# Decode attention on one core: last K block in partition quarters, last turns moved, more of wo before the last V half

## Chip, cores, metric

The kernel runs on 1 core of one Trainium2 chip. The metric is the device time of one execution in microseconds (us), lower is better; quoted times are medians.

## The reference

One decode step: a single query against a long K and V cache, beside a small gated feed-forward part. Cut to what matters here:

```python
# H = 16 heads, Sk = 65536 keys, Dh = 256, D = 448, all bf16
q = (xn @ wq).reshape(B, Sq, H, Dh).transpose(0, 2, 1, 3)
scores = einsum("bhqd,bhkd->bhqk", q, k_cache) * (Dh ** -0.5)
p = softmax(scores, axis=-1)
o = einsum("bhqk,bhkd->bhqd", p, v_cache)
s = o.transpose(0, 2, 1, 3).reshape(B, Sq, H * Dh) @ wo
out = x + s * silu(ffn(xn))          # [1, 1, 448]
```

K and V are 537 MB each. Nearly all the work is to read them once.

## The kernel before

The cache is cut into 64 blocks (16 heads, 4 blocks each) of 128 partitions x 128 keys, 8.4 MB of K and as much of V. Three buffers R0, R1, R2 take the K and V blocks in turn. VectorE and ScalarE form the scores of a block, TensorE multiplies the softmax weights with V, and SyncE issues all large loads into one queue (q1 in the page: 1084.30 of 1084.52 MB). Blocks run in loops; the last ones are written out after them. The parts that the change touches:

```python
def load_keys(T, src, k0, k1, s):
    w = slice(k0 * Dh, k1 * Dh)
    sp.dma_start(out=T[:, w], in_=src[:, w]).then_inc(s, 16)

# after SyncE's loop: K63, V62, V63 and wo, all in one queue
take(sp, vf[0])                                # TensorE has finished with V60 in R0
load_keys(R[0], Kl, 0, HK, kl[0])              # K63, keys 0-63, all 128 partitions
load_keys(R[0], Kl, HK, KB, kh[0])             # K63, keys 64-127
take(sp, kf[2])
for (k0, k1), w in zip(vn, nl):                # V62 in 4 parts
    load_keys(R[2], Vn, k0, k1, w)
take(sp, vf[1])
for (k0, k1), w in zip(vz[:2], zl[:2]):        # V63, first half
    load_keys(R[1], Vl, k0, k1, w)
take(sp, kf[0])                                # VectorE is done with K63's first half
load_wo(0); load_wo(1)                         # wo goes where that half was
for (k0, k1), w in zip(vz[2:], zl[2:]):        # V63, second half
    load_keys(R[1], Vl, k0, k1, w)
load_wo(2); load_wo(3)
# ... (cut)
# TensorE and ScalarE at the end (cut to the order)
keys(psO2, 0, 1, vz, zl, 0, 2, True, od)       # V63 first half
pe_turn()                                      # turns V62's output
project(*pieces[0]); pe_rows(); project(h0, h0 + 3); pe_bcast(); project(h0 + 3, h1)
# ... softmax of the second half, sums, weights
keys(psO, 0, 1, vz, zl, 2, 3, True)
pe_turn()                                      # turns the output of V63's first half
keys(psO, 0, 1, vz, zl, 3, len(vz), False, od)
project(*pieces[2]); pe_turn(tok=True); project(pieces[3][0], H1); project(H1, H)
```

A "turn" is 8 small matmuls that transpose a finished output row; `project` multiplies finished heads with their part of wo.

Of the kernel before, what the change touches and what calls it, by code (L numbers as in the profile page):

```python
# [14 lines left out]
KB = 128  # L15
# [6 lines left out]
def kernel(  # L22
# [25 lines left out]
    LAST = NBLK - 1  # L48
# [19 lines left out]
    pe, dve, act, gp, sp = nc.tensor, nc.vector, nc.scalar, nc.gpsimd, nc.sync  # L68


    KW, HK = KB * Dh, KB // 2

    R = [pool.tile([P, KW], bf16, name=f"R{t}") for t in range(NR)]
# [32 lines left out]
    def rest(n0, n):  # L106
        return R[2][:, n0 : n0 + n], n0 + n

    wq_t, n = rest(0, DF * HD + HD // 2)
    Z, n = rest(n, DX * H * H)  # L110
    w1_t, n = rest(n, DF * F + F // 2)
    w2_t, n = rest(n, FC * D)
    xn, n = rest(n, D)
    xz, n = rest(n, 2 * P)
# [11 lines left out]
    psO, ps_m, ps_nb, ps_t = bank[0][0:2, :], bank[1][:, 0:P], bank[2][:, 0:1], bank[3][:, 0:2]  # L126
    ps_q, ps_y, ps_ao, ps_tot = bank[4][:, 0:Dh], bank[5][0:1, 0:D], bank[6][0:1, 0:D], bank[7]
    psO2, ps_qh = bank[4][0:2, :], bank[3][0:H, 0:Dh]
# [10 lines left out]
    def mark(e, ins):  # L139
        count[e] += 1  # L140
        ins.then_inc(line[e], 1)
        return (e, count[e])

    def need(e, *toks):
        for p, c in toks:
            if seen.get((e, p), 0) < c:
                eng[e].wait_ge(line[p], c)
                seen[(e, p)] = c

    def sem(name):  # L150
        return tc.alloc_semaphore(name)

    def take(e, s, k=1):
        e.wait_ge(s, k).then_inc(s, -k)  # L154

    kl = [sem(f"kl{t}") for t in range(NR)]
    kh = [sem(f"kh{t}") for t in range(NR)]
# [7 lines left out]
    od, oc, ho = sem("od"), sem("oc"), sem("ho")  # L165
# [3 lines left out]
    def cuts(*c):  # L169
        return tuple(zip(c[:-1], c[1:]))  # L170

    vn = cuts(0, 32, 64, 96, 128)
    vz = cuts(0, 32, 64, 96, 112, 120, 128)
    nl = [sem(f"nl{t}") for t in range(len(vn))]
    zl = [sem(f"zl{t}") for t in range(len(vz))]
    pieces = cuts(0, 5, 10, 14, 16)
    wl = [sem(f"wl{t}") for t in range(len(pieces))]

    Kd = A_k_cache[0].rearrange("h (b p c) d -> (h b) p (c d)", p=P, c=KB)
# [3 lines left out]
    def at(n):  # L183
        return slice(n, n + 1) if isinstance(n, int) else bass.ds(n, 1)

    def block(T, i):
        return T[at(i)].rearrange("o p f -> (o p) f")
# [11 lines left out]
# [3 lines that stand above are left out]
# [10 lines left out]
    def dve_gmax():  # L212
        take(dve, tm)
        dve.reduce_max(out=gmax[0:1, :], in_=ps_m[0:1, :], axis=AX.X).then_inc(gm, 1)  # L214


    def dve_block(s, between=None):
        Kv = R[s][:, :].rearrange("p (c d) -> p c d", d=Dh)


        def end(c0, c1, own):
            take(dve, pf, (c1 - c0) // SUB)
            take(dve, sd, own)
            dve.tensor_copy(out=S2[:, c0:c1], in_=S[:, c0:c1]).then_inc(kf[s], 1)  # L224
            dve.reduce_max(out=rmax[:, :], in_=S[:, c0:c1], axis=AX.X).then_inc(rm, 1)  # L225
            if c0 == 0 and between:
                between()
            dve_gmax()

        take(dve, qr)  # L230
        dve.tensor_copy(out=qcur[:, :], in_=ps_q).then_inc(sd, 1)  # L231
        halves = between is not None
        take(dve, kl[s], 16)
        for k in range(NSTEP):
            if k == NSTEP // 2:
                take(dve, kh[s], 16)
            pair = Kv[:, k * SUB + ND : (k + 1) * SUB, :]
            m = dve.tensor_tensor(  # L238
                out=pair,
                in0=pair,  # L240
                in1=qcur[:, None, :].to_broadcast([P, NA, Dh]),
                op=ALU.mult,
            )
            if k == 0:
                m.wait_op(sd, 1, "sem-ge")
            m.then_inc(mr, 1)
            for j in range(ND):
                c = k * SUB + j
                ins = dve.tensor_tensor_reduce(  # L249
                    out=Kv[:, c, :],  # L250
                    in0=Kv[:, c, :],
                    in1=qcur[:, :],
                    scale=1.0,
                    scalar=0.0,
                    op0=ALU.mult,
                    op1=ALU.add,
                    accum_out=S[:, c : c + 1],
                )
            if k == NSTEP - 1:
                ins.then_inc(sd, 1)  # L260
                end(KB // 2 if halves else 0, KB, 1 if halves else 2)
            elif halves and k == NSTEP // 2 - 1:
                ins.then_inc(sd, 1)
                end(0, KB // 2, 2)

    def act_sums(s, k):
        take(act, mr)
        for j in range(NA):
            c = k * SUB + ND + j
            prod = R[s][:, c * Dh : (c + 1) * Dh]  # L270
            ins = act.activation(  # L271
                out=prod,
                in_=prod,
                func=ACT.Identity,
                accum_out=S[:, c : c + 1],
            )
        ins.then_inc(pf, 1)

    def act_softmax(e, s, c0=0, c1=KB):
        def col(a, b):  # L280
            return hist[:, at(e + 2), a:b].rearrange("p o s -> p (o s)")

        take(act, bm)
        act.mul(out=col(0, 1), in_=ps_nb, mul=-scale).then_inc(sa, 1)  # L284
        take(act, sa)
        act.activation(  # L286
            out=PV[s][:, c0:c1],
            in_=S2[:, c0:c1],
            func=ACT.Exp,
            bias=col(0, 1),  # L290
            scale=scale,
            accum_out=col(1, 2),
        ).then_inc(pv, 1)

    def act_out(po=psO):
        take(act, od)
        act.copy(out=O[:, :], in_=po).then_inc(oc, 1)  # L297
# [5 lines left out]
    def act_row(e):  # L303
        take(act, ho)
        return act.copy(out=hist[:, at(e + 2), 2:4].rearrange("p o s -> p (o s)"), in_=ps_t)  # L305
# [35 lines left out]
    def pe_turn(tok=False):  # L341
        take(pe, oc)
        Ov = O[:, :].rearrange("r (j p a) -> r j a p", j=2, a=2)
        for a in range(2):
            for j in range(2):
                ins = pe.matmul(  # L346
                    ps_t[:, a : a + 1],
                    lhsT=Ov[:, j, a, :],
                    rhs=eye2[:, j : j + 1],
                    start=(j == 0),  # L350
                    stop=(j == 1),
                )
        return mark("pe", ins) if tok else ins.then_inc(ho, 1)
# [36 lines left out]
    with tc.tile_critical():  # L390
# [18 lines left out]
        Kl, Vn, Vl = block(Kd, LAST), block(Vd, LAST - 1), block(Vd, LAST)  # L409
# [3 lines left out]
            sp.dma_start(out=wo_t[:, h0:h1, :], in_=wo_d[:, h0:h1, :]).then_inc(w, 16)  # L413

        take(sp, vf[0])
        load_keys(R[0], Kl, 0, HK, kl[0])
        load_keys(R[0], Kl, HK, KB, kh[0])
        take(sp, kf[2])
        for (k0, k1), w in zip(vn, nl):
            load_keys(R[2], Vn, k0, k1, w)  # L420
# [18 lines left out]
        for T, w in ((ident, P), (eye2, 2)):  # L439
# [19 lines left out]
        t = mark("dve", dve.tensor_scalar(  # L459
            out=xn,  # L460
            in0=x_f[0:1, :],
            scalar1=mv[0:1, 0:1],
            scalar2=rstd,
            op0=ALU.subtract,
            op1=ALU.mult,
        ))
# [50 lines left out]
        t = mark("pe", ins)  # L517
# [165 lines left out]
        def keys(po, t, s, cut, sems, a, b, start, done=None):  # L683
            for n in range(a, b):
                (k0, k1), last = cut[n], n == b - 1
                pe.wait_ge(sems[n], 16)
                pe_keys(po, t, s, k0, k1, start and n == a, last and done is not None,
                        done if last else None)
# [3 lines left out]
        keys(psO, 2, 2, vn, nl, 3, 4, False, od)  # L692
        pe_bcast()
        act_softmax(LAST, 0, 0, HK)
        act_sums(0, 2)
        act_out()
        act_sums(0, 3)
        act_row(LAST - 1)


        take(pe, pv)
        keys(psO2, 0, 1, vz, zl, 0, 2, True, od)
        pe_turn()
        need("pe", t_o)
        pe.wait_ge(wl[0], 16)
        project(*pieces[0])
# [3 lines left out]
        project(h0, h0 + 3)  # L710
        pe_bcast()
        project(h0 + 3, h1)
        act_softmax(LAST + 1, 0, HK, KB)

        take(pe, pv)
        t15 = pe_sums(ps_m[:, 0:NL], N1, NENT)
        weights(N1, NENT, H1, H, (ps_m[:, 0:NL], t15))
        act_out(psO2)
        keys(psO, 0, 1, vz, zl, 2, 3, True)
        pe_turn()  # L720
        t_g = silu(g_t, ps_y, g_e, t_y)
        t = mark("act", act_row(LAST))
        need("dve", t)
        outputs(N1, NENT - 1, H1, H, NL - 1)
        keys(psO, 0, 1, vz, zl, 3, len(vz), False, od)
        act_out()
        pe.wait_ge(wl[2], 16)
        project(*pieces[2])
        t = pe_turn(tok=True)
# [12 lines left out]
        t = mark("pe", project(H1, H))  # L742
        need("dve", t, t_g)
        t = mark("dve", dve.tensor_tensor(out=g_t, in0=ps_ao, in1=g_t, op=ALU.mult))  # L744
        need("dve", t)
        t = mark("dve", dve.tensor_tensor(  # L746
            out=x_f[0:1, :], in0=g_t, in1=x_f[0:1, :], op=ALU.add
        ))
# [32 lines left out]
```

## Time and profile before

| | before |
|---|---|
| time, median of the first 3 runs | 2525.48 us |
| span of the profiled run | 2523.2 us |
| read from HBM | 1084.29 MB, 430 GB/s over the span |
| K63: from first issue to last landing | 23.2 us |
| last K63 landing to the end of TensorE's last matmul | 53.3 us |
| VectorE's pause before block 63 | 6.8 us |

K63 was issued at 2442.65 and had landed at 2465.85; TensorE's last matmul ended at 2519.14. The prediction below shows the DMA row of the page, the chain of waits and the ends of the timelines. The table by stretches of time, here while K63 loads (stretch, length, busy time of each engine, granted TensorE clock, busy share of the DMA engines, GB/s):

```profile
2447.00:2460.00 13.00, 12.17 (x59) 4.88 (x57) 10.75 (x52) 8.76 (x44) 0.00 (x0) 1.00 0.95 410
```

TensorE's timeline at the first matmuls on V62 (start, length, engine, line, what, count, and in brackets the idle time before and what ended it):

```profile
2460.84 1.07 PE L346 MATMUL bank<-eye,O 2*128 2x1 f32 x8 [1.30 <-PEq L154]
2470.98 9.37 PE L318 MATMUL bank<-R,PV 128*2 128x512 bf16 x32 [9.08 <-DMA R<-in_A_v_cache_dram]
```

K63 passes at 410 GB/s, and TensorE waits 9.08 us for V62, which is queued behind it.

### The profile page before, as it was taken

Reading aid. Unit: us, or ns where it says so; the run is one execution under the profiler, and the core shown is the slowest. Engines: PE = TensorE matmul, PEld = TensorE weight load, DVE = VectorE, ACT = ScalarE, POOL = GpSimd, SP = SyncE. Lnnn points to the kernel's source line nnn. Section 1 sums busy time; section 2 is a strip of 40 time slices with the busy share of each in tenths; the row PEclk is TensorE's granted clock in tenths of the full one; section 3 lists DMA queues with packets and bytes.
Section 4 is the critical chain, followed back from the end, with each engine's and each line's share of the span. In section 5 each row is a group of like instructions: output and inputs, shape, how many; then the busy total and the mean of one; then the engine's idle time right before and its main releaser. Section 6 shows DMA issues by size and latency. Waiting matters only on the chain. (4 is left out here: it accounts for less than half of the span.)

```text
span 2523.2 us, 29918 instructions
## 1 busy us (share of the span) xinstructions
PE 1198.1 (47%) x5125; PEld 500.5 (20%) x5125; DVE 2233.7 (89%) x10281; ACT 1443.9 (57%) x6992; POOL 2.5 (0%) x13
## 2 busy tenths in 40 slices
PE   3353543534535435445354354454553543534556
PEld 2121211212212112112121121221221211212222
DVE  6989889889899898898898988988989889889886
ACT  3656556556555565565565655655656556556554
POOL 0000000000000000000000000000000000000000
PEclk7676767767767767677676676676766767767778
DMA  9999999999999999999999999999999999999998
GB/s 423 417 430 433 434 431 433 433 432 432 432 432 432 433 434 437 434 435 433 433 433 432 432 432 432 432 433 434 439 434 433 433 433 433 432 432 432 432 412 346
DMA packets 22728, 1084.52 MB, mean 430 GB/s; under 512 B 2354, under 2 KB 4532, under 8 KB 4916
## 3 DMA queue, kind: packets, MB, share of 16 engines
q1 hardware_dynamic: 22706, 1084.30, 99.5%
q8 instruction: 6, 0.10, 0.0%
q14 instruction: 14, 0.11, 0.0%
q10 hardware_dynamic: 2, 0.00, 0.0%
HBM read 1084.29 MB, written 0.00 MB: 430 GB/s over the span
## 5 line engine op out<-in xcount | busy, mean ns | idle before, releaser
L271 ACT ACTIVATE R<-R 128x256 bf16<-128x256 bf16 x3328 | 1330.7, 401 | 697.1 <-ACTq L154 697.1
L249 DVE CUSTOM_DVE_ANT_0 R<-R,qcur 128x256 bf16<-128x256 bf16 x4864 | 1700.2, 417 | 0.0
L318 PE MATMUL bank<-R,PV 128*2 128x512 bf16 x4096 | 1023.7, 416 | 32.4 <-DMA R<-in_A_v_cache_dram 15.3
L238 DVE TENSOR_TENSOR R<-R,qcur 128x3328 bf16<-128x3328 bf16 x256 | 482.6, 1885 | 198.7 <-DVEq L154 198.6
L271 ACT ACTIVATION_READ_ACCUMULATOR R<-R 128x1 f32 x3328 | 620.2, 186 | 2.6 <-issue 2.6
L330 PE MATMUL bank<-ident,rmax 128*1 128x128 bf16 x65 | 17.1, 263 | 1021.6 <-PEq L154 1021.6
L318 PEld LDWEIGHTS bank<-R,PV 128*2 128x2 bf16 x4096 | 365.0, 90 | 663.1 <-issue 208.0
L249 DVE DVE_READ_ACCUMULATOR2_ANT S<- 128x1 f32 x4864 | 383.5, 79 | 0.0
L346 PE MATMUL bank<-eye,O 2*128 2x1 f32 x536 | 98.0, 300 | 236.8 <-PEq L154 236.8
L330 PEld LDWEIGHTS bank<-ident,rmax 128*1 128x1 bf16 x65 | 5.2, 79 | 1026.1 <-issue 1025.9
L346 PEld LDWEIGHTS bank<-eye,O 2*128 2x128 f32 x536 | 94.2, 257 | 254.8 <-issue 254.8
L284 ACT ACTIVATE hist<-bank 128x1 f32 (+1 forms) x65 | 11.1, 171 | 203.4 <-ACTq L154 203.4
L305 ACT COPY hist<-bank 128x2 f32 (+1 forms) x66 | 10.5, 160 | 120.0 <-ACTq L154 120.0
L214 DVE TENSOR_REDUCE gmax<-bank 1x1 bf16<-1x128 f32 x65 | 18.2, 281 | 36.2 <-DVEq L154 36.2
L231 DVE CAST qcur<-bank 128x256 bf16<-128x256 f32 x64 | 27.2, 425 | 20.2 <-DVEq L154 18.3
L297 ACT COPY O<-bank 2x512 f32<-2x512 f32 x67 | 37.5, 559 | 9.1 <-ACTq L154 9.1
L286 ACT ACTIVATE PV<-S,hist 128x128 bf16<-128x128 f32 (+1 forms) x65 | 26.0, 400 | 13.4 <-ACTq L154 13.1
L358 PE MATMUL bank<-q,ident 16*128 16x256 bf16 x63 | 24.4, 387 | 0.0
L224 DVE COPY S<-S 128x128 f32<-128x128 f32 (+1 forms) x65 | 14.7, 226 | 9.5
L225 DVE TENSOR_REDUCE rmax<-S 128x1 bf16<-128x128 f32 (+1 forms) x65 | 18.2, 279 | 0.0
L336 PE MATMUL bank<-gmax,ones_row 1*128 1x1 bf16 x65 | 10.3, 158 | 15.9 <-PEq L154 15.9
L336 PEld LDWEIGHTS bank<-gmax,ones_row 1*128 1x128 bf16 x65 | 6.5, 99 | 33.3 <-issue 33.3
(65 smaller groups left out, 101.7 us busy)
## 6 DMA issues: line engine op xcount, KB each, us to landing
R<-in_A_k_cache_dram SPq DMA_DIRECT2D x4, 4096.0 KB, 23.4
R<-in_A_v_cache_dram SPq DMA_DIRECT2D x7, 2048.0 KB, 23.1
R<-in_A_wq_dram SPq DMA_DIRECT2D x1, 3072.0 KB, 12.7
R<-in_A_wo_dram SPq DMA_DIRECT2D x2, 1120.0 KB, 17.5
R<-in_B_w_dram SPq DMA_DIRECT2D x1, 1568.0 KB, 27.2
R<-in_B_w_dram SPq DMA_DIRECT2D x1, 1344.0 KB, 5.8
R<-in_A_v_cache_dram SPq DMA_DIRECT2D x1, 1024.0 KB, 15.8
R<-in_A_v_cache_dram SPq DMA_DIRECT2D x2, 512.0 KB, 17.0
```

The lines of the kernel that those rows point to most:

```text
L214: dve.reduce_max(out=gmax[0:1, :], in_=ps_m[0:1, :], axis=AX.X).then_inc(gm, 1)
L225: dve.reduce_max(out=rmax[:, :], in_=S[:, c0:c1], axis=AX.X).then_inc(rm, 1)
L231: dve.tensor_copy(out=qcur[:, :], in_=ps_q).then_inc(sd, 1)
L238: m = dve.tensor_tensor(out=pair, in0=pair, in1=qcur[:, None, :].to_broadcast([P, NA, Dh]), op=ALU.mult,)
L249: ins = dve.tensor_tensor_reduce(out=Kv[:, c, :], in0=Kv[:, c, :], in1=qcur[:, :], scale=1.0, scalar=0.0, op0=ALU.mult, op1=ALU.add, accum ...
L271: ins = act.activation(out=prod, in_=prod, func=ACT.Identity, accum_out=S[:, c : c + 1],)
L286: act.activation(out=PV[s][:, c0:c1], in_=S2[:, c0:c1], func=ACT.Exp, bias=col(0, 1), scale=scale, accum_out=col(1, 2),).then_inc(pv, 1)
L297: act.copy(out=O[:, :], in_=po).then_inc(oc, 1)
L318: ins = pe.matmul(po, lhsT=PV[t][:, c : c + 2], rhs=R[s][:, c * Dh : (c + 2) * Dh], start=(start and c == k0), stop=(stop and c == k1 - 2),)
L330: pe.matmul(ps_m[0:1, :], lhsT=rmax[:, 0:1], rhs=ident[:, :], start=True, stop=True).then_inc(tm, 1)
L346: ins = pe.matmul(ps_t[:, a : a + 1], lhsT=Ov[:, j, a, :], rhs=eye2[:, j : j + 1], start=(j == 0), stop=(j == 1),)
L358: pe.matmul(ps_q, lhsT=ident[0:H, at(h)].to_broadcast([H, P]), rhs=q16[:, :], start=True, stop=True,).then_inc(qr, 1)
```

## The change

The intent, as I read it: shorter transfers of K63, so that other traffic gets between them; and less work for TensorE after the last V part lands, by doing turns and projections in its earlier pauses. Loops and arithmetic are unchanged.

```diff
--- before.py
+++ after.py
@@ -170,10 +170,12 @@
         return tuple(zip(c[:-1], c[1:]))
 
     vn = cuts(0, 32, 64, 96, 128)
-    vz = cuts(0, 32, 64, 96, 112, 120, 128)
+    vz = cuts(0, 32, 64, 80, 96, 112, 120, 128)
     nl = [sem(f"nl{t}") for t in range(len(vn))]
     zl = [sem(f"zl{t}") for t in range(len(vz))]
-    pieces = cuts(0, 5, 10, 14, 16)
+    pieces = cuts(0, 5, 12, 14, 16)
+
+    kr = cuts(0, 32, 64, 96, 128)
     wl = [sem(f"wl{t}") for t in range(len(pieces))]
 
     Kd = A_k_cache[0].rearrange("h (b p c) d -> (h b) p (c d)", p=P, c=KB)
@@ -230,10 +232,11 @@
         take(dve, qr)
         dve.tensor_copy(out=qcur[:, :], in_=ps_q).then_inc(sd, 1)
         halves = between is not None
-        take(dve, kl[s], 16)
+        n = 16 * len(kr) if halves else 16
+        take(dve, kl[s], n)
         for k in range(NSTEP):
             if k == NSTEP // 2:
-                take(dve, kh[s], 16)
+                take(dve, kh[s], n)
             pair = Kv[:, k * SUB + ND : (k + 1) * SUB, :]
             m = dve.tensor_tensor(
                 out=pair,
@@ -413,8 +416,9 @@
             sp.dma_start(out=wo_t[:, h0:h1, :], in_=wo_d[:, h0:h1, :]).then_inc(w, 16)
 
         take(sp, vf[0])
-        load_keys(R[0], Kl, 0, HK, kl[0])
-        load_keys(R[0], Kl, HK, KB, kh[0])
+        for (c0, c1), sm in zip(cuts(0, HK, KB), (kl[0], kh[0])):
+            for p0, p1 in kr:
+                load_keys(R[0][p0:p1, :], Kl[p0:p1, :], c0, c1, sm)
         take(sp, kf[2])
         for (k0, k1), w in zip(vn, nl):
             load_keys(R[2], Vn, k0, k1, w)
@@ -692,15 +696,18 @@
         keys(psO, 2, 2, vn, nl, 3, 4, False, od)
         pe_bcast()
         act_softmax(LAST, 0, 0, HK)
+        act_out()
         act_sums(0, 2)
-        act_out()
+        act_row(LAST - 1)
         act_sums(0, 3)
-        act_row(LAST - 1)
 
 
         take(pe, pv)
-        keys(psO2, 0, 1, vz, zl, 0, 2, True, od)
+        keys(psO2, 0, 1, vz, zl, 0, 1, True)
         pe_turn()
+        keys(psO2, 0, 1, vz, zl, 1, 2, False, od)
+        act_out(psO2)
+        act_softmax(LAST + 1, 0, HK, KB)
         need("pe", t_o)
         pe.wait_ge(wl[0], 16)
         project(*pieces[0])
@@ -710,19 +717,16 @@
         project(h0, h0 + 3)
         pe_bcast()
         project(h0 + 3, h1)
-        act_softmax(LAST + 1, 0, HK, KB)
+        pe_turn()
 
         take(pe, pv)
         t15 = pe_sums(ps_m[:, 0:NL], N1, NENT)
         weights(N1, NENT, H1, H, (ps_m[:, 0:NL], t15))
-        act_out(psO2)
-        keys(psO, 0, 1, vz, zl, 2, 3, True)
-        pe_turn()
+        t_r = mark("act", act_row(LAST))
         t_g = silu(g_t, ps_y, g_e, t_y)
-        t = mark("act", act_row(LAST))
-        need("dve", t)
+        need("dve", t_r)
         outputs(N1, NENT - 1, H1, H, NL - 1)
-        keys(psO, 0, 1, vz, zl, 3, len(vz), False, od)
+        keys(psO, 0, 1, vz, zl, 2, len(vz), True, od)
         act_out()
         pe.wait_ge(wl[2], 16)
         project(*pieces[2])
```

## The prediction

> **What bounds the kernel now.** I read four views of the kernel before, widest first. The page shows what fills the span:
>
> ```profile
> DMA  9999999999999999999999999999999999999998
> HBM read 1084.29 MB, written 0.00 MB: 430 GB/s over the span
> L249 DVE CUSTOM_DVE_ANT_0 R<-R,qcur 128x256 bf16<-128x256 bf16 x4864 | 1700.2, 417 | 0.0
> ```
>
> All 40 slices of the DMA row are full. VectorE is busy for 89% of the span, but it too waits for transfers. The diff touches nothing in the loops, so only the last 80 us, after K block 63 is issued, can move. The chain of work that ended last, in order of time (start, us, what), says what ends the program:
>
> ```profile
> 2484.34 23.09 DMA R<-in_A_v_cache_dram
> ...
> 2507.47 3.61 PE bank L318 x16
> 2511.08 1.03 PE bank L346 x8
> 2512.11 3.54 PE bank L318 x16
> 2515.66 1.51 PE bank L662 x8
> 2517.17 1.03 PE bank L346 x8
> 2518.20 0.95 PE bank L662 x4
> ...
> 2519.18 0.62 DVE R L744
> 2519.82 0.61 DVE x_f L746
> ```
>
> The last V half lands while wo is still arriving; then TensorE alone needs 11.67 us (3.61+1.03+3.54+1.51+1.03+0.95) to 2519.15, VectorE 1.23, and the output transfer 2.8 to the span's end at 2523.2. Third, the timelines of VectorE and TensorE in that stretch:
>
> ```profile
> 2458.56 0.28 DVE L214 TENSOR_REDUCE gmax<-bank 1x1 bf16<-1x128 f32 x1 [0.94 <-DVEq L154]
> 2465.61 0.42 DVE L231 CAST qcur<-bank 128x256 bf16<-128x256 f32 x1 [6.77 <-DVEq L154]
> ...
> 2503.67 0.22 PE L330 MATMUL bank<-ident,rmax 128*1 128x128 bf16 x1 [0.49 <-PEq L154]
> 2507.47 3.61 PE L318 MATMUL bank<-R,PV 128*2 128x512 bf16 x16 [0.99 <-DMA R<-in_A_v_cache_dram]
> ```
>
> VectorE stands 6.77 us between block 62 and block 63. It does not wait for data: the query matmul (L358) ended at 2458.62, and the two K63 transfers, issued from 2442.65, landed after 12.0 and 22.8 us, so the first half was in SBUF at 2454.65. Fourth, the line view of L201 there, and the DMA queues from 2463.7 to 2465.7:
>
> ```profile
> DMA to landing us min/median/max: 12.0/17.4/22.8
> ...
> q14 instruction: 1, 0.01, 1.0%
> ```
>
> From 2458.7 to 2463.7 that view shows only the data queue. One 8 KB instruction transfer runs at 2463.76, just as an engine ends its rows of the second K63 half, and VectorE resumes 1.5 us after it. I read the stall as an instruction fetch after the loop[...].
>
> [...] a 128-partition K63 half gives each engine 8 rows of 32 KB at 1.213 us (from the transfer records), 9.7 us in a row, and the fetch enters at its end.
>
> [...] The trace before has no transfer of 32 partitions that could test this; it shows only the full rate, 32 KB in 1.213 us on each of 16 engines, 432 GB/s[...].[...]
>
> **The change part by part.**
>
> 1. Quarters of K63: two transfers of 4 MB become eight of 1 MB. At 0.38 us per issue this adds 6 x 0.38 = 2.3 us to SyncE, which next has work at 2457.5: hidden. [...] 8.39 MB take 38.8 us instead of 19.4 (8.39 MB / 432 GB/s). Everything behind is in the same queue: V62 (8.39 MB), V63 (8.39), wo (3.67). It arrives 19 us later.
>
> VectorE barely cares: the first half would land at 2443.6 + 19.4 = 2463, before it now starts (2465.6), and the second at 2482, where it starts the second half at 2486.2. The cost sits purely on the transfers.
>
> 2. More wo early: piece 1 grows from 5 to 7 heads. Two heads are 2 x 229 KB = 0.46 MB, 1.07 us at 430 GB/s. All later V63 parts land 1.07 us later; the last wo byte is unmoved. Four projection matmuls (about 0.85 us) leave the end.
>
> 3. Smaller first parts of the last V half: 32 keys (4.9 us of transfer) become 16+16. The first lands 2.44 us earlier than the 32 would, 1.37 net of part 2. One more issue (about 0.45 us), hidden, SyncE being some 17 us ahead.
>
> 4. Turns: V62's turn moves between the parts of V63's first half, and that half's turn (1.03 us) moves from the final stretch into the wait for the last half. ScalarE's copies move ahead to suit. The number of matmuls does not change.
>
> At full rate the sum is: wo piece 1 lands at 2502.5 + 1.07 = 2503.6; TensorE then runs its 14 projection matmuls (2.9), a turn (1.0), and the sums (0.4), to about 2508.0. The first 16 keys landed at 2506.0, so it runs 32 key matmuls of 0.2255 back to back: 7.2, to 2515.2. Then four projections 0.85, turn 1.03, last projections 0.95: 2518.0, instead of 2519.15. That is 1.1 us. VectorE restarting some 3.7 us sooner (2458.8 + 1.2 mean wait + 0.3 + 1.5 = 2461.9, not 2465.6) gives TensorE at most 0.5 more before landings bind. So parts 2 to 4 with a shorter fetch are worth 1 to 2 us: 2524.
>
> At half rate: the last wo piece, issued at about 2496.8 and landed 19.1 us later at 2515.9, lands at about 2515.9 + 19 = 2534.9. TensorE has caught up with its transfers by then; after the landing there are 0.95 of projections, 1.23 of VectorE and 2.8 of output, so the span ends at 2539.9, 16.7 above 2523.2. About 2.4 us of the old chain thus hides under the delay. Some lag of single engines at the old end (1 to 3 us between the first engine and the last) may go, so I take 15.5: 2541.
>
> **The rivals.**
>
> A, my main case: the eight quarters run at half rate in turn, 2541. [...] Against: [...] whoever split by partition rather than by key must have expected something of it.
>
> B: quarters cost nothing[...]. Then the fetch gets in sooner and the tail shrinks: 2524. For it: the 6.77 us stall is real[...]. Against: VectorE's restart is not on the chain that ended last; the 23.09 us transfer is. So even then little comes of it.
>
> C: partial overlap. The engines start K63 staggered by up to 0.7 us and may drift apart[...]. With 300 GB/s K63 takes 28 us, 8.6 late; TensorE's 3 us of backlog absorbs part, and the time is about 2531.
>
> D: the fetch stays as long[...]. This changes VectorE by 2 to 3 us, but with A's delay nothing at the end.
>
> **Range and chances.** I give A 0.62, B 0.26, C 0.12. A spans 2537 to 2545, B 2522.5 to 2525.5. A range for eight in ten must hold both, 2522.5 to 2544; the centre is weighted to A with a little of C: 2538. Either way it is well under 2% (50 us): faster 0.005, same 0.985, slower 0.01.
>
> **What would show each step.** Right under A: the K63 quarters of the first half land up to some 20 us after issue and the second up to 39; a stretch from 2444 to 2482 shows about 215 to 230 GB/s; TensorE's first V62 matmul moves from 2470.98 to about 2489; the chain ends in a wait for wo or the last V part, followed by only a few matmuls. Right under B: the same stretch shows 430 GB/s, the cast at L231's successor starts at about 2462, TensorE's last matmul ends at about 2518, and the chain keeps about 32 key matmuls after the last wait. A new idle of TensorE before a turn or the projections would show step 4 wrong. The prediction as a whole fails if the quarters cost more than half the rate, or if the time falls below 2522.

Three things stand as assumptions. First, that quarters of 32 partitions run at half rate: 38.8 us is twice the 19.4 that the trace gives for K63. On it the sum of case A came to a span of 2539.9, 16.7 us above 2523.2, and with 15.5 in place of 16.7 to a time of 2541. Second, that a fetch enters once an engine has ended its rows of one transfer, as the one fetch seen did. With quarters the longest wait would then be two rows of 1.213 us, 2.4 us; half of it is the "1.2 mean wait" in the full-rate sum, which came to 2518.0 for TensorE's end and 2524 for the time. Third, in rival D, that the fetch waits as long as before because two rows at half rate take 4.9 us.

## The result

The changed kernel takes 2545.13 us (2543.87 to 2547.67, 6 runs) against 2525.47 (2525.04 to 2528.47, 6 runs). The ratio is 1.0077, 95% interval 1.0064 to 1.009. The change costs some 20 us, clearly, though less than the 2% that counts as slower. The prediction was 2538 with a range up to 2544: the right direction and the right class, 1.1 us outside the range.

The page of the changed kernel. The DMA row and the GB/s row have one figure for each fortieth of the span:

```profile
DMA  9999999999999999999999999999999999999998
GB/s 419 415 428 431 431 435 436 430 433 439 431 429 436 438 429 433 439 431 430 438 435 429 434 439 430 429 442 432 429 436 437 430 431 441 431 429 440 433 284 337
HBM read 1084.29 MB, written 0.00 MB: 426 GB/s over the span
```

The DMA row is the same, digit for digit, as before. The loss shows only in GB/s: slice 39 falls to 284, where the kernel before has 412. The same stretch in the table by stretches:

```profile
2447.00:2460.00 13.00, 13.00 (x62) 5.05 (x61) 11.83 (x59) 10.25 (x52) 0.00 (x0) 1.00 0.97 202
```

The DMA engines are as busy as before (0.97 against 0.95) and move half as much (202 GB/s against 410). In the transfer records a row of 32 KB takes 2.55 us in place of 1.213 (medians of K63's 256 rows). The eight K63 loads, from issue to landing in the line view of L203, where the two of before took 12.0 and 22.8 us:

```profile
DMA to landing us min/median/max: 7.6/24.4/40.4
```

The timeline of VectorE, then that of TensorE (the line numbers are 2 or more higher than before):

```profile
2460.59 0.28 DVE L216 TENSOR_REDUCE gmax<-bank 1x1 bf16<-1x128 f32 x1 [1.62 <-DVEq L154]
2470.54 0.42 DVE L233 CAST qcur<-bank 128x256 bf16<-128x256 f32 x1 [9.66 <-DVEq L154]
...
2506.97 0.28 DVE L216 TENSOR_REDUCE gmax<-bank 1x1 bf16<-1x128 f32 x1 [13.68 <-DVEq L154]
```

```profile
2493.38 13.39 PE L321 MATMUL bank<-R,PV 128*2 128x512 bf16 x48 [29.43 <-DMA R<-in_A_v_cache_dram]
...
2518.72 5.30 PE L321 MATMUL bank<-R,PV 128*2 128x512 bf16 x16 [1.12 <-DMA R<-in_A_v_cache_dram]
2523.86 2.06 PE L666 MATMUL bank<-R,OT 128*1 128x448 bf16 x10
2525.75 0.22 PE L333 MATMUL bank<-ident,rmax 128*1 128x128 bf16 x1
2525.87 1.30 PE L666 MATMUL bank<-R,OT 128*1 128x448 bf16 x6
2527.10 0.17 PE L339 MATMUL bank<-gmax,ones_row 1*128 1x1 bf16 x1
2527.20 1.68 PE L666 MATMUL bank<-R,OT 128*1 128x448 bf16 x8
2528.80 1.10 PE L349 MATMUL bank<-eye,O 2*128 2x1 f32 x8
2529.83 0.39 PE L653 MATMUL bank<-hist,ones_sq 128*128 128x5 f32 x2
2530.15 7.07 PE L321 MATMUL bank<-R,PV 128*2 128x512 bf16 x32
2537.05 0.92 PE L666 MATMUL bank<-R,OT 128*1 128x448 bf16 x4
2538.05 1.07 PE L349 MATMUL bank<-eye,O 2*128 2x1 f32 x8
2539.05 1.01 PE L666 MATMUL bank<-R,OT 128*1 128x448 bf16 x4
```

TensorE now waits 29.43 us for V62 instead of 9.08. VectorE's pause before block 63 grew from 6.77 to 9.66 us, and a new one of 13.68 appeared: its next step needs a small TensorE matmul (L333, at 2506.61) that stands behind the late V62 keys (2493.38 to 2506.77) in TensorE's order. At the end, once the last bytes of V63's first half have come (2518.72), TensorE's matmuls run to 2540.06 without any pause. Their first 16 took 5.30 us instead of 3.61 before, at a granted clock of 0.68 in that stretch against 1.00. Even so TensorE was not late at the end: the weight load (PEld) of the four projections at 2537.05 still had to wait for a part of wo:

```profile
2537.00 0.52 PEld L666 LDWEIGHTS bank<-R,OT 128*1 128x1 bf16 x4 [0.29 <-DMA R<-in_A_wo_dram]
```

The profiled spans differ by 2544.16 - 2523.24 = 20.9 us. I split this at the landings of K63:

| stretch, us | before | after | difference |
|---|---|---|---|
| start of the span to the first K63 issue | 2442.65 | 2444.68 | +2.0 |
| K63 issue to last K63 landing | 23.2 | 43.75 | +20.55 |
| last K63 landing to the end | 57.38 | 55.73 | -1.65 |

The first row lies before anything that the change touches; it is the spread between two executions. The medians, which average over it, differ by 19.7.

### The profile page after: what moved, and what is told of

It reads as the page before. It is cut to its first block, busy times and chain, and to the rows that moved or that the text cites. A ratio compares the mean times of both kernels' runs of the same rounds, so it can differ in the third digit from the quotient of the medians. Undisturbed runs are those within 1.5% of the kernel's fastest.

```text
span 2544.2 us, 29925 instructions
## 1 busy us (share of the span) xinstructions
PE 1204.5 (47%) x5125; PEld 502.8 (20%) x5125; DVE 2233.6 (88%) x10281; ACT 1443.5 (57%) x6992; POOL 2.5 (0%) x13
## 5 line engine op out<-in xcount | busy, mean ns | idle before, releaser
L333 PE MATMUL bank<-ident,rmax 128*1 128x128 bf16 x65 | 17.1, 263 | 1019.2 <-PEq L154 1019.2
L333 PEld LDWEIGHTS bank<-ident,rmax 128*1 128x1 bf16 x65 | 5.2, 79 | 1023.5 <-issue 1023.1
```

Of the source, the lines that this page charges most:

```text
L333: pe.matmul(ps_m[0:1, :], lhsT=rmax[:, 0:1], rhs=ident[:, :], start=True, stop=True).then_inc(tm, 1)
```

## The experiments

**Theory and rivals.** My theory: a transfer over 32 or 64 neighbouring partitions runs at half rate, one over 16 at a quarter, one over partitions spread over the whole range at the full rate, and nothing overlaps a slow one. No trace had shown why that should be so; it is an assumption that the runs test. In the expectations below, the forecast before each rival is the theory's. Rivals: small or numerous transfers are slow; the order of the quarters is at fault; the loss needs the other parts of the change. A second question is what the instruction fetch behind VectorE's pause waits for (that the pause is such a fetch is my reading; in all twelve traces an 8 KB instruction transfer runs in it and VectorE goes on 1.5 to 2.0 us after its end). The fetch theory is the prediction's second assumption: it enters where an engine has ended its rows of one transfer, since the one in the trace before ran at 2463.76, just after the first such ends (2463.62). A third question is what parts 2 to 4 are worth. Ten kernels ran, all correct. The first four shared one chip and 9 runs of the kernel before (2526.32); the second four another and 7 runs (2526.65); the last two one run (2526.26).

### Quarters undone, the rest kept

```diff
-    kr = cuts(0, 32, 64, 96, 128)
+    kr = cuts(0, 128)
```

> The changed kernel with only the quarters undone: each half of K block 63 is again one transfer over all 128 partitions. [...] K63 again takes about 20 us at 430 GB/s and the time is 2524, 1 to 2 us below the kernel before. Rival (the rest of the change costs time, for instance the reordered turns or the larger wo piece): the time stays several us above the kernel before, 2530 or more.

Measured: 2525.03 us, ratio 0.9996 (0.9983 to 1.001), which the interval does not tell from no change. K63 took 23.3 us. The whole loss is in the quarters. In the trace, last K63 landing to TensorE's end is 52.0 us against 53.3 before: the rest of the change does save about 1.3 us there, too little for the runs to show.

### Quarters alone, on the kernel before

```diff
-        load_keys(R[0], Kl, 0, HK, kl[0])
-        load_keys(R[0], Kl, HK, KB, kh[0])
+        for (c0, c1), sm in zip(cuts(0, HK, KB), (kl[0], kh[0])):
+            for p0, p1 in kr:
+                load_keys(R[0][p0:p1, :], Kl[p0:p1, :], c0, c1, sm)
     # and the waits of 16 on kl[0], kh[0] become 16 * len(kr)
```

> The kernel before with only the quarters added. [...] K63 takes some 42 us, as in the changed kernel, and the time is 2545 to 2547, at or 1 to 2 us above the changed kernel because the old end of the program is kept. Rival (quarters are harmless alone, the loss needs the new order): 2525.

Measured: 2545.85 us, ratio 1.0077 (1.0061 to 1.0092), the same as the whole change. From the last K63 landing to TensorE's end it took 51.75 us, as good as the changed kernel's 51.6: in these two executions the old end is in total no worse than the new. In this execution K63 was issued 5 us earlier, behind a V61 that was still loading, so issue to landing (48.6) is not comparable; the last byte landed at 2485.96, 20.1 later than before.

### Same number of transfers, cut by keys instead of partitions

```diff
-            for p0, p1 in kr:
-                load_keys(R[0][p0:p1, :], Kl[p0:p1, :], c0, c1, sm)
+            for t in range(len(kr)):
+                w = (c1 - c0) // len(kr)
+                load_keys(R[0], Kl, c0 + t * w, c0 + (t + 1) * w, sm)
```

> The changed kernel with each K63 half cut into four transfers of 16 keys over all 128 partitions instead of four of 32 partitions: as many transfers, of the same 1 MB each. [...] full rate, 430 GB/s over K63, time 2523 to 2525. Rival (eight small transfers, or two waits for four, cost the time): about 2545 as in the changed kernel. Fetch theory[...]: VectorE's pause before block 63 shrinks from 6.8 us to 5 or less, because an engine has 2.4 us of one transfer in a row instead of 9.7; if the fetch waits for something else, the pause stays at 6 to 7 us.

Measured: 2524.59 us, ratio 0.9999 (0.9985 to 1.0012), K63 in 23.2 us. The table by stretches of this run:

```profile
2447.00:2460.00 13.00, 12.46 (x60) 5.02 (x58) 10.89 (x54) 8.78 (x45) 0.00 (x0) 1.00 1.01 424
```

Eight transfers of 1 MB run at 424 GB/s, so neither size nor number is at fault. But VectorE's pause hardly shrank:

```profile
2465.19 0.42 DVE L233 CAST qcur<-bank 128x256 bf16<-128x256 f32 x1 [6.07 <-DVEq L154]
```

6.07 us, where the fetch theory wanted 5 or less. The run with eight pieces by keys, below, has more on this.

### Halves of 64 partitions

```diff
-    kr = cuts(0, 32, 64, 96, 128)
+    kr = cuts(0, 64, 128)
```

> The changed kernel with two pieces of 64 partitions per K63 half instead of four of 32: transfers of 2 MB, 4 rows per engine. [...] K63 runs at the same 200 to 215 GB/s and the time is again about 2545. Rival (the fixed cost of each transfer, or the two rows per engine, make the loss): half as many transfers, so about half the loss, 2534.

Measured: 2544.6 us, ratio 1.0073 (1.0057 to 1.0088), K63 in 44.1 us:

```profile
2447.00:2460.00 13.00, 12.28 (x60) 4.93 (x57) 11.02 (x54) 8.76 (x44) 0.00 (x0) 1.00 0.99 205
```

Half as many transfers with twice the partitions run at the same 205 GB/s. So 64 neighbours give no more than 32 did (202 GB/s), as the theory had it.

### Eighths of 16 partitions

```diff
-    kr = cuts(0, 32, 64, 96, 128)
+    kr = cuts(0, 16, 32, 48, 64, 80, 96, 112, 128)
```

> The changed kernel with eight pieces of 16 partitions per K63 half instead of four of 32. [...] a row of 32 KB takes about 5.1 us instead of 2.55, K63 about 82 us, and the time is some 40 us above the changed kernel, about 2585. Rival (a transfer over fewer than 128 partitions runs at half rate whatever its count; the runs with 32 and 64 partitions gave the same): the time stays at 2545.

Measured: 2574.82 us, ratio 1.0168 (1.0128 to 1.0207; the interval includes 2%, so the verdict is unclear whether this is slower by that much). Half the partitions again halves the rate, nearly (113 GB/s against 202):

```profile
2447.00:2460.00 13.00, 11.96 (x58) 4.78 (x56) 10.62 (x52) 8.76 (x45) 0.00 (x0) 1.00 0.98 113
```

The rival of one fixed half rate falls. The size of my estimate was off: a row took some 4.4 us rather than 5.1 and K63 73.9 rather than 82. One of the four executions took only 2556.79; it was not profiled, so why is open.

### Quarters in alternating order

```diff
-    kr = cuts(0, 32, 64, 96, 128)
+    kr = ((0, 32), (64, 96), (32, 64), (96, 128))
```

> The changed kernel with the quarters issued in the order 0-31, 64-95, 32-63, 96-127[...]. If all engines go through the queue in step (my theory), [...] about 2545, at most 3 us less for the half row by which the engines are apart. Rival (the order is at fault, [...] alternating lets them overlap): K63 near 430 GB/s, about 2525.

Measured: 2545.01 us, ratio 1.0073 (1.0056 to 1.009), K63 in 43.2 us, 212 GB/s in the same stretch. Order does not help: K63 took 43.75 us in the changed kernel, so at most a small part of one transfer overlaps the next. That the engines go through the queue in step is my reading of this; no view shows the engines one by one.

### Quarters of every fourth partition

```diff
-            for p0, p1 in kr:
-                load_keys(R[0][p0:p1, :], Kl[p0:p1, :], c0, c1, sm)
+            for t in range(len(kr)):
+                load_keys(R[0][t::4, :], Kl[t::4, :], c0, c1, sm)
```

> The changed kernel with each quarter made of every fourth partition (0, 4, 8, ... and so on) instead of 32 neighbours: as many transfers, rows and bytes[...]. If only the set of partitions of a transfer counts: full rate, 2524 to 2526. [...] If the destination is not addressed as written, the result is wrong and the run only counts for its time.

Measured: correct, 2525.3 us, ratio 0.9992 (0.9975 to 1.0008):

```profile
2447.00:2460.00 13.00, 12.86 (x60) 4.92 (x58) 11.46 (x58) 6.60 (x34) 0.00 (x0) 0.98 1.00 430
```

This is the sharpest of the tests. Number, size, row length and partition count of the transfers are those of the changed kernel; only which 32 partitions go together differs. The rate is 430 GB/s and a row takes 1.213 us. The loss comes from taking neighbours (202 GB/s). One rival is untested: `Kl[t::4]` also takes other rows of HBM together than before, and no run changes the HBM rows or the partitions alone. Whether the limit lies at the partitions that are written or at the addresses in HBM that are read is not shown. The theory did forecast that 64 neighbours are no faster than 32 (205 against 202 GB/s) and 16 about half as fast (113), but that is a pattern and not a cause. My second guess, that even such a set would run at half rate (about 2545), was wrong; how the partitions are dealt to the engines no run shows.

### Sixteen pieces by keys, for the fetch

```diff
     # on the run cut by keys
-    kr = cuts(0, 32, 64, 96, 128)
+    kr = cuts(0, 16, 32, 48, 64, 80, 96, 112, 128)
```

> The kernel with K63 cut by keys, now in eight pieces of 8 keys per half (512 KB, 4 KB rows, all partitions). For VectorE's pause before block 63, which was 6.8 us with whole halves and 6.1 with pieces of 16 keys. If the fetch waits for the border of a transfer, the pause falls to about 3 us (1.2 us of one transfer at a time, and 1.8 for the fetch itself). If it waits behind a fixed amount of queued data on its engine, the pause stays near 6 us. The time itself should be 2524 to 2526, as the pause is not on the chain that ends last.

Measured (one execution): 2525.13 us.

```profile
2466.41 0.42 DVE L233 CAST qcur<-bank 128x256 bf16<-128x256 f32 x1 [5.97 <-DVEq L154]
```

The pause is 5.97 us with transfers of 1.2 us per engine, 6.07 with 2.4 and 6.84 with whole halves. (The 1.2 and 2.4 are estimates: 512 KB and 1 MB over 16 engines at 32,768 B per 1.213 us.) Against the fetch theory there is also the last run below (turns and larger wo piece), whose K63 comes in whole halves: its pause is as short, so the smaller pieces cannot be said to have shortened it at all.

```profile
2464.95 0.42 DVE L233 CAST qcur<-bank 128x256 bf16<-128x256 f32 x1 [5.74 <-DVEq L154]
```

There the fetch started at 2463.08, 0.9 us before the first engine wrote the 4-byte mark that ends its rows of the second half. So the fetch did not wait for the border of a transfer. I measured the time from the start of the pause to the start of the 8 KB instruction transfer, in the transfer records:

| K63 cut into | a row of 32 KB takes, us | pause starts to fetch starts, us | at that rate, KB of data per engine |
|---|---|---|---|
| whole halves (before) | 1.213 | 4.9 | 133 |
| whole halves (turns and larger wo piece) | 1.213 | 3.9 | 105 |
| 16 keys | (8 KB rows, full rate) | 4.1 | 110 |
| 8 keys | (4 KB rows, full rate) | 4.0 | 107 |
| every fourth partition | 1.213 | 3.9 | 106 |
| 32 neighbours (after) | 2.55 | 7.2 | 93 |
| 16 neighbours | 4.4 | 15.5 | 115 |

(The last column is the wait times 32,768 bytes over the row time, in thousands of bytes; the rows by keys use 1.213.) The waits vary fourfold, the amounts stay between 93 and 133 KB (87 and 135 over all twelve traces). Whole halves alone scatter from 105 to 135, which covers the cuts by keys. That fits a fetch that waits behind a roughly fixed amount of queued data on its engine. It is a fit, not a proof: no run set that amount.

### Parts 2 to 4 one by one

Both build on the run with the quarters undone.

```diff
-    vz = cuts(0, 32, 64, 80, 96, 112, 120, 128)
+    vz = cuts(0, 32, 64, 96, 112, 120, 128)
-    pieces = cuts(0, 5, 12, 14, 16)          # turns only
+    pieces = cuts(0, 5, 10, 14, 16)          # (kept at 0, 5, 12, 14, 16 in the second run)
```

> The changed kernel with the quarters, the larger wo piece and the smaller V parts all undone: only the turns of the last outputs and ScalarE's copies are moved. Measured from the landing of the last K63 byte to TensorE's last matmul, which took 53.3 us before and 52.0 with all three (whole K63). If the moved turn is what saves: about 52.6, since one turn of 1.0 us leaves the end and TensorE loses its 1 us wait before the last half. If the smaller pieces save instead: 53.3 as before.

> As the run with only the turns moved, plus the larger wo piece, still without the smaller V parts. By my working the larger piece delays the first 32 keys of the last half by 1.1 us, which TensorE then waits for again, while 4 projections (0.85 us) leave the end: the two cancel, 52.7. If wo ahead pays by itself: 51.8.

Measured, one execution each: 2527.91 and 2525.16 us. The second took 52.8 us from the last K63 landing to TensorE's end, near the 52.7 of my working, and it shows the wait that I had put there:

```profile
2509.04 7.07 PE L321 MATMUL bank<-R,PV 128*2 128x512 bf16 x32 [0.57 <-DMA R<-in_A_v_cache_dram]
```

With the smaller V parts as well this wait is gone and the figure is 52.0. The run with the turns only is inconclusive. It took 56.2 us, because VectorE started block 63 only at 2468.00 in that execution, 2.4 us later than before, and TensorE then waited for it:

```profile
2506.06 0.22 PE L333 MATMUL bank<-ident,rmax 128*1 128x128 bf16 x1 [2.45 <-PEq L154]
```

The run with every fourth partition shows the same: there K63 was in SBUF at 2463.12, 2.7 us earlier than before, and TensorE waited 2.44 us for VectorE at this place instead, so the time did not fall. In these runs the transfers and VectorE are within 2 to 3 us of each other at the end.

No version beat the kernel before beyond the interval. All that keep the rate lie between 0.9992 and 0.9999 of it, with 1 inside each interval.

## Why the prediction was right and wrong

**Part 1, the quarters: right in kind.** The main case A said half rate, in turn, with everything behind it late. Its signs appeared: 206 GB/s from 2444 to 2482 (215 to 230 forecast), landings up to 40.4 us after issue (39), V62's first matmul at 2493.4 (2489). Only the last did not come as written: the chain view shows no wait, and the wait for wo in the PEld line above is followed by 4 projections, a turn and 4 projections. The runs with 64, 32 and 16 neighbours (205, 202 and 113 GB/s) and with every fourth partition (430) show that the loss comes from which partitions go together, though not why; the run with the quarters undone and the run with the quarters alone show that nothing else in the change costs time beyond the interval. Rival B falls with the result itself, rival C also with the alternating order, which gave no overlap either.

**Its size was too small.** The working took exactly half rate, 19.4 us more. A row took 2.55 us, 5% more than twice 1.213, and K63 grew by 20.55 us. So the prediction's own sign of failure, that the quarters cost more than half the rate, came true by that little. (Smaller slips: its half-rate sum goes on with 19 us where it had worked out 19.4, VectorE's restart adds up to 2461.8 and not 2461.9, and the last of the 40 DMA slices stands at 8, not 9.)

**The step that failed** is the term that took the added 19 us down to 15.5: "after the landing there are 0.95 of projections", so that "2.4 us of the old chain" hide under the delay, and some 1.2 us of lag of single engines goes. After the last K63 landing the program became only 1.65 us shorter, not 3.5.

- The path was wrong. The working took the last wo part as what ends the program. It landed at 2538.07, and TensorE ended at 2540.06, 2.0 us later and not 0.95. The part of wo before it, landed at 2536.96, has more work behind it: 4 projections, a turn and 4 projections, 3.1 us. TensorE "has caught up with its transfers by then" was right, as the weight load that waits for this part shows. In all seven runs with the whole new end and no late VectorE, delayed or not, TensorE ends 3.0 to 3.2 us after this landing. With the quarters undone it ends 2.1 us after the last wo landing, with them 2.0: the delay itself hides 0.1 us at most. The rest of the 1.3 us gained against the kernel before (3.3) comes from the new end.
- The lag was too large: from the last K63 landing to the last wo landing it took 49.6 us against 50.0 before, 0.4 less instead of 1.2.

A was 2541; with 20.55 and 1.65 in place, 2525.5 + 18.9 = 2544.4, which the 2545.13 confirms within the spread of runs.

**The range was also set wrongly.** A was given up to 2545, yet the range for the mixture stopped at 2544, and its centre was pulled to 2538 by rivals that did not happen.

**"VectorE barely cares" was wrong**, though it cost nothing by itself. The pause grew instead of shrinking, by rival D's amount (2.9 us against 2 to 3) but not for its reason (cuts by keys leave the pause at 6.07 and 5.97 us), and the 13.68 us wait behind V62 was not foreseen: V62 late means TensorE late (by 29.43 us of waiting), and VectorE's maximum needs TensorE. That VectorE's restart is off the chain held for the kernel before by a small margin only, as the runs with a late VectorE show.

**Parts 2 to 4: right at full rate.** The sum put TensorE's end at 2518.0; with the quarters undone it was 2517.98. That the larger wo piece pays only together with the smaller V parts is supported by a single execution. Under the quarters, these parts save nothing in total (51.6 against 51.75). After the last wo landing the new end is 1.1 us shorter there too (2.0 against 3.05 in the run with the quarters alone), but in that run the transfers from the last K63 landing to the last wo landing took 0.9 us less (48.7 against 49.6); with one trace of each, that may be scatter.

**The longest wait of 2.4 us for a fetch** (the second assumption, half of it in the sum) was wrong: transfers of 2.4 and 1.2 us left a wait of 4.1 and 4.0. That the fetch in the trace before entered just as an engine ended its rows was a coincidence, as the run with whole halves and a fetch 0.9 us before any such end shows.

## What to carry to other kernels

When a load is cut into smaller transfers, cut by keys within each partition (424 GB/s here), or take partitions spread over the whole range (every fourth: 430); a run of 32 or 64 neighbouring partitions halved the rate here (202 and 205) without the DMA engines looking less busy (0.97 and 0.99), so read GB/s and not the busy share. In the full queue here, what one slow load lost was paid by everything behind it, nearly in full: with the quarters alone the last K63 byte landed 20.1 us later, and the time rose by 19.5 (2545.85 against 2526.32). Before crediting a delay with hiding later work, check that the later work depends on something other than the delayed data, and follow the last landings one by one: the last need not be the one with the longest work behind it.
